# Fourteen idle products during the weight load, and a new issue order planned with later transpose landings

## The chip, the cores and the metric

The kernel runs on one core of a Trainium2 chip. The metric is device time in microseconds (us) of one execution. Before the change the median of five runs was 1848.56 us, from 1846.41 to 1852.45.

## What is computed

The input `x` has 2048 rows of 512 numbers. Four blocks follow one another, A, B, A, B, each added to its own input after a layernorm. All weights are shared between the two layers.

```python
def _A_ref(x, mem0, Wq, Wk, Wv, Wo, seg_len):      # 32 heads of 128, M = 8, seg_len = 32
    mem = mem0
    for s in range(n_seg):                          # 64 segments
        xs = x[:, s * seg_len:(s + 1) * seg_len, :]
        h = jnp.concatenate([mem, xs], axis=1)      # 40 rows
        q, k, v = (jnp.einsum('btd,dhe->bhte', h, W) for W in (Wq, Wk, Wv))
        p = softmax(where(mask, q k^T * scale, -1e9))
        o = jnp.einsum('bhte,hed->btd', p v, Wo)
        mem = o[:, :M, :]                           # the next segment's first 8 rows
        outs.append(o[:, M:, :])

def _B_ref(x, wqkv, wo):                            # linear attention, 32 heads of 16
    ...
    kv = jnp.einsum('bhsd,bhse->bhde', pk, v)       # summed over all 2048 rows
    ...
```

Block A is a recurrence: the eight memory rows of a segment are the first eight output rows of the segment before it. So 64 segments in each of two layers, 128 in all, follow one another. Block B needs a sum over all rows before any of its outputs can be made.

## The kernel before

**Work.** The weights of block A stay in SBUF (`Wq_sb`, `Wk_sb`, `Wv_sb`, 4 MB each, and `Wo_sb`). They are loaded at the start: the ACT queue issues the loads of Wq, Wk and Wv one after the other, and the SP queue issues four loads of Wo, two of them only when Wk has landed and two when Wv has landed. `wqkv` of block B follows on SP after the last of Wo.

A tile `t` (or `G`) is 128 rows of x, so four segments. A segment `s` multiplies a block of 32 rows: 8 memory rows and the first 24 of its own rows. The 8 rows that are left of each of the four segments of a tile are put together as a "left" block of 32 rows and done once a tile, ahead of need (`left_block`). Heads are done in two halves `b`. The steps of a segment:

- `turned` projects a block by Wq or Wk (through `project`, L777: 16 products of 32 columns by 512, four to a PSUM tile's four column groups), copies the result to an image `img` in SBUF (L608 on ACT or L609 on DVE), and turns it to have the head's dimension on the partitions. For half 0 of segments 1 to 62, and for both halves of the left block, the turning is a DMA transpose issued from SP (L790). For the others it is 16 transposing products (L799) and a copy. The image ring has three places for the segments' own images (marked urgent), and a fourth place alone for the left block, so the next left image can be copied only when the last one's transpose has landed.
- `project` by Wv gives `vimg`.
- `mem_attention(s, b)` makes the memory rows' attention: scores (L861), exponential, masks, sums (L878), and the product with v (L891, L892).
- `out_block` multiplies by Wo (L987, in `out_proj`), `next_mem` (L1012) turns the result into the next segment's memory rows in `hT`.
- `x_attention` (L916, L932, L935, L959, L960) and `residual` (L1029) do the other rows. `left_block` has the left block's own scores at L827. `prepare` does the layernorm (L738 to L750) of the next tile and its left block.
- `b_in`, `b_mid` and `b_out` are block B's parts, put between the segments; `b_mid` and the work around it stand alone between the layers.

**Order.** Nothing is issued in the order in which it is written. Each operation becomes a node with a cost in us; a node that issues a DMA has also a landing time `lat`. `_Prog.schedule` then goes through simulated time: each engine takes, among the nodes that are ready by the plan, the one with the highest priority. The priority of a node is

```python
                step, name, k = nd.key
                nd.prio = -(step * PERIOD + OFFSET[name][k])
```

so the table `OFFSET` is the order: some 350 numbers, one for each operation of a segment, written out. `MODE_SLACK` says how much priority TensorE gives away to stay in the same tiling mode of the array, and `LOOK` for how long it is kept free for a product of higher priority that is about to be ready. The planner also gives out the eight PSUM banks. What it yields is a fixed order of instructions on each engine, with semaphore waits where one engine needs another. On the chip each engine goes through its list in order; the plan's times do not exist there, only the order does. An instruction that waits holds up all behind it on its engine.

**What the plan assumed of DMAs.** A transpose is held to occupy SP for 1.25 us and to land `TURN` = 1.8 us later, so 3.05 us from its issue. The loads of rows of x are held to land 2.0 us after their issue. The weights are held to land 13.2, 23.7 and 34.8 us after theirs.

Of the kernel before, what the change touches and what calls it, by code (L numbers as in the profile page):

```python
# [16 lines left out]
HOP = 0.06  # L17
PE_SWITCH = 0.1
TURN = 1.8
MODE_SLACK = 12.41  # L20

LOOK = 0.074

PERIOD = 13.5
OFFSET = {
    "ld0": (3.45,),
    "ld1": (4.20,),
    "ld2": (-0.95,),
    "ld3": (-2.85,),
    "ld4": (0.40,),  # L30
    "startF": (12.05,),
    "prepF": (-11.05, 4.70, -9.25, -18.05, -7.00, -0.35, -15.95, -12.35, -15.40, 1.00, -1.65),
    "left0F": (-15.70, 1.30, -14.50, 0.25, -0.65, -12.60, 1.65, 6.55),
    "left1F": (15.35, 7.60, -6.60, 4.95, -3.45, 3.20, -0.65, 3.10),
    "leftv0F": (-1.70, -10.10),
    "leftv1F": (9.60, 0.00),
    "leftsF": (3.55, 9.85, 9.35, 1.25),
    "xlF": (1.05,),
    "qk0F": (0.15, 4.00, 2.75, -11.15, 1.55, 1.85, 11.40, 4.05),
    "qk1F": (0.00, -3.50, -2.10, -1.25, -25.90, -0.00, -5.45, 1.95),  # L40
    "v0F": (10.40, 1.50),
    "v1F": (31.95, 7.50),
    "mem0F": (2.55, 0.25, 5.85, -8.30, -1.20, -6.05, 2.15, 3.05, -1.60),
    "mem1F": (17.30, 12.60, 0.00, 1.10, -1.45, -6.00, -2.05, -21.65, 0.45),
    "outF": (1.85, -6.05, -5.85, -2.60),
    "nextF": (-0.45, -5.40, 13.70),
    "xF": (8.05, 1.50, -5.55, 5.05, -0.25, 9.95, 19.65, 5.95, -2.30, 7.20, 8.70, -12.05, -8.75, 4.00, -1.15,
        37.05, 0.30, 2.95, 10.30, 7.45, -2.10, 1.40, 0.10),
    "qk0": (-14.10, 1.50, -0.25, -5.35, -0.10, -0.05),
    "qk1": (1.55, 4.60, -0.05, -0.60, 1.80, 0.00, 7.10, -0.45),  # L50
    "v0": (0.35, -0.20),
    "v1": (5.15, 3.10),
    "mem0": (-5.20, -2.15, -1.60, -49.45, -13.55, -22.95, -3.35, -7.90, 4.70),
    "mem1": (7.10, -4.05, 3.25, -3.75, -2.90, 12.50, 5.15, -16.25, -12.15),
    "out": (-0.75, 4.95, 2.15, 0.00),
    "next": (1.75, 2.45, -4.05),
    "res": (48.90, 6.30, 2.30, -15.10, -1.45, -7.60, -2.50),
    "x": (2.45, 5.90, -2.85, -0.45, 6.20, 0.00, 15.70, -4.55, -22.30, 6.10, -15.10, 5.80, -2.55, 10.75, 6.10,
        0.60, 3.80, 21.60, 10.55, 5.20, 22.60, 29.30, 0.00),
    "prep": (7.35, -10.90, 1.30, 0.30, 10.40, -17.80, -4.90, 5.95, -3.00, -10.50, 9.70),  # L60
    "left0": (-4.00, -0.25, 18.45, -8.00, 1.40, -0.65),
    "left1": (0.10, 3.65, 0.45, 20.95, 3.05, -3.60),
    "leftv0": (32.60, 0.10),
    "leftv1": (11.30, 2.45),
    "lefts": (-2.95, 4.00, 0.50, -7.85),
    "xl": (6.35,),
    "bi": (0.25, -5.75, -1.85, -4.15, 6.60, -10.30, 9.70, -1.75, -6.35, 0.00, -15.35, 2.10, 7.40, -0.60, 21.85,
        -3.30, -3.50, 3.75, 0.00, 7.95, 2.05, 2.85, 12.85),
    "qk0L": (-9.45, 1.80, -2.10, 2.25, -3.65, 4.55, -0.30, 0.30),
    "qk1L": (-2.85, -6.75, -3.35, 4.40, -6.30, 2.10, -0.10, -1.70),  # L70
    "xL": (-6.30, -9.90, -7.95, -2.90, -3.60, 0.00, 4.70, 0.70, -2.85, 14.90, -19.10, 0.15, -0.20, 1.10, 6.60,
        0.15, -2.50, -0.30, -0.90, 0.00, -4.35),
    "lr": (-0.80, 7.55, 8.15, -13.30, 0.15, 7.95),
    "outL": (15.55, 3.95, 0.40, 10.10),
    "resL": (1.40, 4.60),
    "biL": (4.55, -5.70, -1.45, -34.70, -5.20, 0.75, 5.85, -1.90, -1.35, 0.15, 2.50, -24.50, -0.65, -21.55,
        1.05, 0.00, 0.00, 5.40, -1.60, -1.10, 11.15, -3.20, 3.85),
    "bm": (-3.95, -5.05, 16.55, 0.70, -0.20, 3.70, -9.00, 16.45, 0.15, -8.55, 2.25, 4.05, 2.75),
    "boF": (0.00, 7.10, -11.80, 3.35, 0.85, 0.75, -24.50, -13.85),
    "bo": (-1.10, 6.15, -2.70, -2.90, 0.00, -11.50, 1.10, -9.70),  # L80
    "ldL": (22.20, 1.70),
    "boL": (-26.60, 4.05, -1.85, -7.50, -5.65, -6.10, -13.50),
    "boZ": (18.15, -34.85, -14.20, 0.00, 8.30, -5.35, -7.10),
}


# [12 lines left out]
def c_pe(n_mm, n):  # L99
    return n_mm * max(0.0255, (n / 2.4 + 3.0) * 1e-3)  # L100
# [390 lines left out]
def _build_kernel(nc, A_x, A_mem0, A_Wq, A_Wk, A_Wv, A_Wo, A_seg_len, B_wqkv, B_wo, out):  # L491
# [34 lines left out]
    x_sb = sb("x_sb", [128, NX, D])  # L526
# [93 lines left out]
    o_view = out[0].rearrange("(t p) d -> t p d", p=128)  # L620
    qk_view = [W.rearrange("(c p) h e -> p c (h e)", p=128) for W in (A_Wq, A_Wk, A_Wv)]

    def x_move(o, i, k, reads, writes, kind, eng="pool"):
        add(eng, lambda e: e.dma_start(o, i), 1.1 if eng == "pool" else 0.4, reads=reads, writes=writes,
            dsem="%s%d" % (kind, k), lat=2.0)

    shift = [0]

    def slot(t):

        return (t + shift[0]) % NX
# [1 line left out]
    P.at(-9000, "ld0")  # L633
    add("sp", lambda s: s.dma_start(mem0_sb[0:M, :], A_mem0[0]), 0.1, writes=[MEM0], dsem="dmem", lat=2.0)
    P.at(-8000, "ld1")
    add("sp", lambda s: s.dma_start(x_sb[:, 0, :], x_view[0]), 0.4, writes=[("x", 0)], dsem="dx0", lat=2.0)
    late = []
    for i, (W, v, nm, t) in enumerate(((Wq_sb, qk_view[0], "Wq", 13.2), (Wk_sb, qk_view[1], "Wk", 23.7),
                                       (Wv_sb, qk_view[2], "Wv", 34.8))):
# [81 lines left out]
    def _m0(t, tl=tl):  # L721
        for c in range(4):
# [3 lines left out]
    evac(memT0_sb[:, :, :], lambda tl=tl: tl.bf16()[:, 0:4 * M].rearrange("p (c m) -> p c m", m=M), 32, tiles=[tl],  # L726
         writes=["memT0"])


    ln_no = [0]  # L730

# [30 lines left out]
    def a_layer(base, first):  # L762
# [20 lines left out]
        def turned(W, key, blk, bkeys, b, dst, dkey, urgent, dma):  # L783

            tl = project(W, key, blk, bkeys, b, urgent)
            k = img_no[0] % NI if urgent else NI
            img_no[0] += urgent
            nd = evac(img[:, k, :], lambda: tl.f32()[:, :], 512, tiles=[tl], writes=[("img", k)], urgent=urgent)
            if dma:
                add("sp", lambda e: e.dma_start_transpose(dst.rearrange("p h j x -> p h (j x)"), img[:, k, :]), 1.25,  # L790
                    reads=[("img", k)], writes=[dkey], dsem="turn%d" % k, lat=TURN)
                return nd
            tt = P.tile()

            def tr(pe):
                for i in range(4):
                    for j in range(4):
                        o = 128 * i + 32 * j
                        r = pe.transpose(tt.bf16()[32 * j:32 * j + 32, 128 * i:128 * i + 128], img[:, k, o:o + 32],  # L799
                                         id_sb[:, :], tile_position=(0, 32 * j))  # L800
                return r
            add("pe", tr, c_pe(4, 128), reads=[("img", k), "id"], tiles=[tt], urgent=urgent, mode="col")
            evac(dst.rearrange("p h j x -> p (h j x)"), lambda: tt.bf16()[:, 0:512], 512, tiles=[tt], writes=[dkey],
                 rate=2, urgent=urgent)
            return nd
# [193 lines left out]
        def out_block(s):  # L999
            at(s, "out")  # L1000
            keys = [[("oTm", s % NO, b), ("oTx", s % NO, b)] for b in range(2)]
            return out_proj(oTb[:, s % NO, :, :], keys, True)
# [61 lines left out]
        def tokens(t, s):  # L1064

            if not first:
                b_out(base + s, t, 0)
            elif t:
                at(s, "xl")
                x_move(x_sb[:, slot(t), :], x_view[t], slot(t), [], [("x", slot(t))], "dxl")  # L1070

        at(-4, "start")
        evac(hT[:, 0, 0, :, 0:8], memT0_sb[:, :, :], 32, reads=["memT0"], writes=[("hTm", 0, 0)])
# [3 lines left out]
        for s in range(NSEG):  # L1077
            G, g = divmod(s, 4)
            r2 = s % 2
            blk = hT[:, G % 2, g, :, :]  # L1080
            bk = [("hTm", G % 2, g), ("hTx", G % 2, g)]
            if g == 0 and G + 1 < NT:
                tokens(G + 1, s)
            for b in range(2):
                at(s, "qk%d" % b)
                hs = slice(4 * b, 4 * b + 4)
                turned(Wq_sb, "Wq", blk, bk, b, qT[:, r2, hs, :, :], ("qT", r2, b), True, QDMA[b] and 0 < s < NSEG - 1)
                turned(Wk_sb, "Wk", blk, bk, b, kT[:, r2, hs, :, :], ("kT", r2, b), True, KDMA[b] and 0 < s < NSEG - 1)
            for b in range(2):
                at(s, "v%d" % b)  # L1090
                tl = project(Wv_sb, "Wv", blk, bk, b, True)
                evac(vimg[:, r2, 512 * b:512 * b + 512], lambda tl=tl: tl.f32()[:, :], 512, tiles=[tl],
                     writes=[("v", r2, b)], urgent=True)
            if s + 1 < NSEG:
                for b in range(2):
                    mem_attention(s, b)
            w_of[s] = out_block(s)
            if s + 1 < NSEG:
                next_mem(s, w_of[s])
            if s > 0:  # L1100
                residual((s - 1) // 4, (s - 1) % 4, w_of[s])
                if g == 0:
                    b_in(base + s + 2, G - 1, not first)
            x_attention(s)
            if g == 2 and G + 1 < NT:
                prepare(G + 1, s)
            if s == NSEG - 1:
                at(s, "lr")
                add("pool", lambda p: p.memset(oTl[:, :, 24:32], 0.0), 0.5, writes=[("oTl", b) for b in range(2)])
                left_rows(NT - 1)  # L1110
# [206 lines left out]
```

The softmax here doesn't subtract the row's maximum and nothing guards it: scores larger than these inputs give would overflow.

## Time and profile before

| what | value |
|---|---|
| median of five runs | 1848.56 us |
| the profiled execution | 1852.73 us |
| its span, first to last instruction | 1851.0 us |
| around the span | 1.7 us |
| mean granted TensorE clock | 0.989 |
| PE busy | 1759.0 us, 95% of the span |
| ACT, DVE busy | 1207.7 us, 1017.4 us |
| matrix products recorded | 46693 |
| DMA transposes | 368 |

The profile is one execution. PE is TensorE's products, PEld its weight loads, DVE VectorE, ACT ScalarE, POOL GpSimd, SP the queue that issues the transposes. "L790" is line 790 of the kernel before. The lines of the helpers stand for many operations: L608 and L609 are nearly all copies out of PSUM on ACT and DVE. `arena_sb` is the one SBUF tensor that holds all working buffers, so a wait for `arena_sb` must be told apart by its line.

The span has four parts: the start (0 to about 100 us, in which the weights land), 64 segments of the first layer up to about 905 us, some 20 us between the layers in which one operation waits for the other, 64 segments of the second layer up to about 1811 us, and an end of 40 us.

### The profile page before, as it was taken

How to read it: one execution, taken by the hardware profiler on the slowest of the kernel's cores; microseconds unless marked ns; L12 is line 12 of the kernel's file. 1: busy time of each engine (PE TensorE's matmuls, PEld its weight loads, DVE VectorE, ACT ScalarE, POOL GpSimd, SP SyncE). 2: the span in 40 equal slices, each digit the busy share in tenths (PEclk: the TensorE clock that was granted, in tenths of full speed). 3: DMA queues.
4: the chain of work that ended last, by engine and by line, in shares of the span. 5: the costliest groups of instructions: out<-in, count | busy, mean ns of one | idle time of the engine just before them, and what ended most of it. 6: DMA issues, size and time to landing. Idle time of an engine off the chain costs nothing.

```text
span 1851.0 us, 100858 instructions
## 1 busy us (share of the span) xinstructions
PE 1759.0 (95%) x46693; PEld 1195.3 (65%) x46693; DVE 1017.4 (55%) x3168; ACT 1207.7 (65%) x3127; POOL 77.0 (4%) x182
## 2 busy tenths in 40 slices
PE   5899999999999999999799999999999999999997
PEld 2566666666667666666566666666766666666663
DVE  2355555555555555555545555556555566555565
ACT  3566666766666666666466667666667666667665
POOL 3000000000000000000000000000000000000000
PEclk9999999999999999999899999999999999999998
DMA  9322121212221222211011222122222222122222
GB/s 366 83 39 40 40 41 35 47 37 44 37 38 43 35 46 38 41 40 38 22 26 41 37 38 49 37 41 44 40 37 49 39 45 41 41 42 43 51 64 95
DMA packets 218934, 94.85 MB, mean 51 GB/s; under 512 B 202536, under 2 KB 212656, under 8 KB 216976
## 3 DMA queue, kind: packets, MB, share of 16 engines
q1 hardware_dynamic: 211312, 60.22, 17.9%
q0 software_dynamic: 5616, 15.60, 2.8%
q10 hardware_dynamic: 1584, 12.58, 1.7%
q8 instruction: 365, 5.98, 1.4%
q14 instruction: 57, 0.47, 0.1%
HBM read 29.63 MB, written 10.49 MB: 22 GB/s over the span
## 4 chain that ended last, share of the span: by engine, by line
PE 81%; DMA 13%; ACT 3%; DVE 2%; issue 1%; SPq 0%; ACTq 0%; DVEq 0%
PE pb L777 36%; PE pb L987 16%; DMA arena_sb<-arena_sb 10%; PE pb L861 3%; PE pb L959 3%; PE pb L1029 3%; PE pb L799 3%; PE pb L1137 3%; ACT arena_sb L608 2%; PE pb L916 2%; PE pb L878 2%; PE pb L1173 1%; DMA Wk_sb<-in_A_Wk_dram 1%; PE pb L892 1%; PE pb L891 1%; PE pb L1255 1%
## 5 line engine op out<-in xcount | busy, mean ns | idle before, releaser
L608 ACT ACTIVATE arena_sb<-pb 128x512 bf16<-128x512 f32 (+6 forms) x1412 | 726.8, 523 | 363.1 <-PE pb L777 300.0
L777 PE MATMUL pb<-Wq_sb,arena_sb 128*32 128x512 bf16 x5120 | 357.4, 383 | 0.7 <-DMA Wq_sb<-in_A_Wq_dram 0.6
L777 PE MATMUL pb<-Wv_sb,arena_sb 128*32 128x512 bf16 x5120 | 354.8, 380 | 0.6 <-issue 0.6
L777 PE MATMUL pb<-Wk_sb,arena_sb 128*32 128x512 bf16 x5120 | 344.2, 382 | 6.3 <-DMA Wk_sb<-in_A_Wk_dram 5.5
L987 PE MATMUL pb<-Wo_sb,arena_sb 128*32 128x256 bf16 x10368 | 327.3, 273 | 9.2 <-issue 3.9
L987 PEld LDWEIGHTS pb<-Wo_sb,arena_sb 128*32 128x32 bf16 x10368 | 261.8, 96 | 38.7 <-DVE arena_sb L895 13.2
L944 DVE TENSOR_TENSOR arena_sb<-arena_sb 32x256 bf16<-32x256 bf16 x512 | 213.2, 416 | 120.4 <-ACT arena_sb L940 109.3
L609 DVE CAST arena_sb<-pb 128x128 bf16<-128x128 f32 (+3 forms) x334 | 118.4, 355 | 252.5 <-PE pb L1012 200.7
L609 DVE COPY arena_sb<-pb 128x512 bf16<-128x512 bf16 (+2 forms) x352 | 137.6, 392 | 210.9 <-PE pb L799 205.6
L777 PEld LDWEIGHTS pb<-Wk_sb,arena_sb 128*32 128x32 bf16 x5120 | 142.3, 97 | 125.7 <-DMA Wk_sb<-in_A_Wk_dram 5.6
L777 PEld LDWEIGHTS pb<-Wq_sb,arena_sb 128*32 128x32 bf16 x5120 | 133.5, 97 | 114.0 <-DVE arena_sb L609 24.1
L777 PEld LDWEIGHTS pb<-Wv_sb,arena_sb 128*32 128x32 bf16 x5120 | 134.3, 97 | 85.0 <-issue 2.4
L608 ACT ACTIVATE outW_sb<-pb 128x128 fp32r<-128x128 f32 x261 | 72.4, 277 | 116.7 <-PE pb L987 77.4
L799 PEld LDWEIGHTS pb<-id_sb,arena_sb 128*32 128x32 bf16 x4352 | 77.3, 97 | 96.3 <-ACT arena_sb L608 65.2
L959 PE MATMUL pb<-arena_sb 128*128 128x128 bf16 x1024 | 131.3, 217 | 0.3 <-DVE arena_sb L946 0.3
L799 PE MATMUL pb<-id_sb,arena_sb 128*32 128x128 bf16 x4352 | 109.7, 221 | 19.6 <-ACT arena_sb L608 19.1
L946 DVE TENSOR_TENSOR arena_sb<-arena_sb 32x64 bf16<-32x64 bf16 x512 | 111.0, 217 | 15.8
L960 PE MATMUL pb<-arena_sb 128*128 128x32 bf16 x1024 | 118.7, 178 | 0.0
L868 ACT ACTIVATE arena_sb<-pb 128x256 bf16<-128x256 f32 x252 | 96.1, 383 | 29.4 <-PE pb L861 22.8
L861 PE MATMUL pb<-arena_sb 128*128 128x32 bf16 x2016 | 96.9, 178 | 6.9 <-DMA arena_sb<-arena_sb 6.7
L861 PEld LDWEIGHTS pb<-arena_sb 128*128 128x128 bf16 x2016 | 74.7, 96 | 31.4 <-DMA arena_sb<-arena_sb 7.8
L895 DVE TENSOR_TENSOR arena_sb<-pb,arena_sb 128x128 bf16<-128x128 f32 x252 | 72.2, 286 | 40.1 <-ACT arena_sb L883 27.6
(121 smaller groups left out, 2307.9 us busy)
## 6 DMA issues: line engine op xcount, KB each, us to landing
arena_sb<-arena_sb SPq DMA_TRANSPOSE x368, 2.5
Wq_sb<-in_A_Wq_dram ACTq DMA_DIRECT2D x1, 4096.0 KB, 13.6
Wk_sb<-in_A_Wk_dram ACTq DMA_DIRECT2D x1, 4096.0 KB, 24.4
Wv_sb<-in_A_Wv_dram ACTq DMA_DIRECT2D x1, 4096.0 KB, 34.8
Wo_sb<-in_A_Wo_dram SPq DMA_DIRECT2D x4, 1024.0 KB, 11.7
xs_scratch<-x_sb POOLq DMA_DIRECT2D x32, 128.0 KB, 2.1
pq_scratch<-arena_sb POOLq DMA_DIRECT2D x32, 128.0 KB, 2.8
x_sb<-xs_scratch POOLq DMA_DIRECT2D x16, 128.0 KB, 2.4
```

The source lines that it names most:

```text
L608: return e.activation(o() if callable(o) else o, i() if callable(i) else i, ACTF.Copy)
L609: return e.tensor_copy(o() if callable(o) else o, i() if callable(i) else i)
L777: r = pe.matmul(tl.f32()[32 * j:32 * j + 32, 0:512], blk[:, c, :], W[:, c, o:o + 512], start=(c == 0), stop=(c == 3), tile_position=(0, 32 ...
L799: r = pe.transpose(tt.bf16()[32 * j:32 * j + 32, 128 * i:128 * i + 128], img[:, k, o:o + 32], id_sb[:, :], tile_position=(0, 32 * j))
L861: r = pe.matmul(tl.f32()[:, o:o + 32], kk[:, hh, :, :].rearrange("p j x -> p (j x)"), qT[:, r2, hh, :, 0:8], start=True, stop=True)
L868: add("act", lambda a: a.activation(Pm[:, k, :, :].rearrange("p a q -> p (a q)"), tl.f32()[:, 0:256], ACTF.Exp, scale=SCALE), c_act(256), ...
L895: add("dve", lambda v: v.tensor_tensor(oTb[:, s % NO, 16 * b:16 * b + 16, 0:8], pv.f32()[:, 0:128].rearrange("p (n q) -> p n q", q=8), Rm[ ...
L944: add("dve", lambda v, q=q, j=j: v.tensor_tensor(Pbx[q, :, j, 0:32], Px[q, :, :], Rx[q, :, :], ALU.mult), c_dve(256) + 0.075, reads=["Px", ...
L946: add("dve", lambda v, q=q, j=j: v.tensor_tensor(Pbx[q, :, j, 32:40], PLL[q, g2, :, gl], Rx[q, :, 0:8], ALU.mult), c_dve(64) + 0.075, read ...
L959: pe.matmul(o, vimg[:, r2, e], Pbx[:, hh, :, 0:32], start=True, stop=False)
L960: return pe.matmul(o[:, :, 0:8], vleft[:, g2, e], Pbx[:, hh, :, 32:40], start=False, stop=True)
L987: r = pe.matmul(tl.f32()[32 * j:32 * j + 32, 0:256], oT[:, 4 * hh + n, :], Wo_sb[:, 8 * n + hh, 256 * d:256 * d + 256], start=(hh == 0 and ...
```

## The change

**The products.** After the second node of `mem_attention(0, 1)`, the scores against kT of the very first segment, fourteen products are added. Each has 32 columns of the identity as its weights and 512 columns of Wq as its moving operand, all in one column group of one PSUM tile. Nothing reads the result. Their priority is -2000, so in the plan PE takes them only when it has nothing else that is ready; they need PE, `id`, `Wq`, and one PSUM bank from the first to the last of them.

**The assumed landings.** A transpose is now held to land 0.2 us later when it is a segment's own and 0.6 us later when it is the left block's: 3.25 us and 3.65 us from issue. The first two loads of x are held to land 8.5 us after their issue and not 2.0. These numbers change nothing on the chip by themselves; they change what the planner puts where.

**The order.** Every number of `OFFSET` is new, and so are `MODE_SLACK` and `LOOK`. No operation of the computation is added or taken away.

```diff
-MODE_SLACK = 12.41
+MODE_SLACK = 29.57
 
-LOOK = 0.074
+LOOK = 0.055
 
 PERIOD = 13.5
 OFFSET = {
...
-    "mem0F": (2.55, 0.25, 5.85, -8.30, -1.20, -6.05, 2.15, 3.05, -1.60),
+    "warm": (2000.00,),
+    "mem0F": (3.95, -0.55, -1.40, -2.60, -33.00, 21.50, -6.90, -14.80, -1.80),
...
-    "qk0": (-14.10, 1.50, -0.25, -5.35, -0.10, -0.05),
-    "qk1": (1.55, 4.60, -0.05, -0.60, 1.80, 0.00, 7.10, -0.45),
+    "qk0": (-23.70, 0.00, 0.80, -6.15, 1.50, 2.10),
+    "qk1": (2.90, 1.80, -13.45, 4.95, 1.10, 6.10, -0.00, -5.35),
...
-    "left0": (-4.00, -0.25, 18.45, -8.00, 1.40, -0.65),
-    "left1": (0.10, 3.65, 0.45, 20.95, 3.05, -3.60),
+    "left0": (-0.50, 3.85, -5.00, -2.55, -3.35, 0.30),
+    "left1": (-5.30, -12.45, -0.35, -5.85, -0.70, -2.25),
...
-    "lefts": (-2.95, 4.00, 0.50, -7.85),
+    "lefts": (-7.25, 1.75, 2.50, -1.30),
...
 }
...
-    add("sp", lambda s: s.dma_start(x_sb[:, 0, :], x_view[0]), 0.4, writes=[("x", 0)], dsem="dx0", lat=2.0)
+    add("sp", lambda s: s.dma_start(x_sb[:, 0, :], x_view[0]), 0.4, writes=[("x", 0)], dsem="dx0", lat=8.5)
...
+    def warm(step, n, after):
+
+        P.at(step, "warm")
+        tl = P.tile()
+        for i in range(n):
+            if i:
+                P.again()
+            add("pe", lambda pe: pe.matmul(tl.f32()[0:32, 0:512], id_sb[:, 0:32], Wq_sb[:, 0, 0:512], start=True, stop=True,
+                                           tile_position=(0, 0)),
+                c_pe(1, 512), reads=["id", "Wq"], tiles=[tl], mode="col", after=after if i == 0 else ())
...
-                    reads=[("img", k)], writes=[dkey], dsem="turn%d" % k, lat=TURN)
+                    reads=[("img", k)], writes=[dkey], dsem="turn%d" % k, lat=TURN + (0.2 if urgent else 0.6))
...
-                x_move(x_sb[:, slot(t), :], x_view[t], slot(t), [], [("x", slot(t))], "dxl")
+                x_move(x_sb[:, slot(t), :], x_view[t], slot(t), [], [("x", slot(t))], "dxl", lat=8.5 if t == 1 else 2.0)
...
+            if first and s == 0:
+                warm(0, 14, [n for n in P.nodes if n.key == (0, "mem1F", 1)])
```

## The prediction

> **What bounds the kernel now.** I read the page first, its busy times, slices and chain:
>
> ```profile
> span 1851.0 us, 100858 instructions
> PE 1759.0 (95%) x46693; PEld 1195.3 (65%) x46693; DVE 1017.4 (55%) x3168; ACT 1207.7 (65%) x3127; POOL 77.0 (4%) x182
> PEclk9999999999999999999899999999999999999998
> PE 81%; DMA 13%; ACT 3%; DVE 2%; issue 1%; SPq 0%; ACTq 0%; DVEq 0%
> ```
>
> TensorE is the bound: busy for 95% of the span and 81% of the chain that ended last. The next engine, ACT, stands at 65%. So a change of order gains only where it fills idle time of PE, or lowers the time that PE loses between products of different kinds. How much is idle, and where, comes from busy times by stretch. The second row of the two below is the same for the second layer:
>
> ```profile
> 100.00:900.00 800.00, 779.62 (x21420) 540.53 (x21416) 442.74 (x1401) 542.17 (x1442) 25.24 (x47) 1.00 0.21 39
> 1000.00:1800.00 800.00, 782.65 (x21088) 538.64 (x21076) 462.15 (x1464) 538.90 (x1380) 31.10 (x57) 1.00 0.22 42
> ```
>
> The first number after the length is PE: 20.4 us idle in the first layer's stretch and 17.35 in the second's, 37.7 together, at the full clock. The rest of PE's 92 us of idle time (1851.0 less 1759.0) is 28.4 in the first 100 us, 11.3 in 900 to 1000, 14.6 after 1800. The last two are chains of single operations between and after the layers, which an order cannot shorten much. So the order can win at most about 38 us in the layers, plus something at the start. The waits of PE in the first stretch, longest in sum first, and L827's of the second, show what the 37.7 are:
>
> ```profile
> PE pb L799 <- ACT arena_sb L608: 5.9, 11, 0.8
> PE pb L861 <- DMA arena_sb<-arena_sb: 5.1, 6, 1.1
> PE pb L827 <- DMA arena_sb<-arena_sb: 3.1, 5, 0.9
> ...
> PE pb L827 <- DMA arena_sb<-arena_sb: 4.9, 7, 1.1
> ```
>
> (us in sum, times, longest). L827 waits for transposes of the left block, L861 for those of the segment's own images. L799 waits for a copy on ACT, and I followed each of these one step back: 14 of 23 such copies had themselves waited for the landing of a transpose, because an image place was still being read. By the semaphores each belongs to a segment's own image. In the two stretches, L827 lost 8.1 us (12 times), L861 6.7 (8 times), L799 behind ACT 9.5 (14 times): 24.3 of the 37.7 us of idle time in the layers come from transposes that landed late.
>
> The row of the transposes says how late:
>
> ```profile
> L790 SPq DMA_TRANSPOSE arena_sb<-arena_sb x368: 1188/1210/2526, 37.0 to 1783.1; - x184
> DMA to landing us min/median/max: 2.4/2.5/6.5
> ```
>
> The median, 2.5 us from issue, is under the 3.05 of the old plan. But counted one by one the landings fall in two groups: 210 of 368 are under 2.7 us, and 87 are over 3.65, most between 3.9 and 4.4. All 158 that are over 2.7 overlap with a packet of the instruction queue (the page's queue q8, 365 packets, 5.98 MB); of the 210 fast ones 75 do. So the plan is right or generous for two in three, and about 1 us short for one in four. The chain passes through 46 transposes, 43 of them in the two stretches, none of these under 3.3 us.
>
> **The landings and the order.** The old margin was 3.05 us; the new is 3.65 for the left block's and 3.25 for a segment's own. A consumer that the plan puts 0.6 or 0.2 us later finds that much less of the wait, if other products stand in between, and with PE 97.6% busy in the layers they nearly always do. Taken wait by wait, min(wait, 0.6) over L827's thirteen (one more lies at 975 us) sums to 7.1 us; min(wait, 0.2) over L861's eight is 1.6 and over L799's fourteen 2.7. That is 11.4 us at most from these waits. From below: nothing, if the order only moves them, since which transposes meet an instruction packet is drawn anew with the order. I take the left block's in full, 7.1, as nothing in the recurrence waits for a left block that is worked a tile ahead, and half of the segment's own, 2.2, since those are in the recurrence. Sum: -9.3.
>
> The segment's own transposes can also cost. In 62 segments of each layer the plan now has the memory scores 0.2 us later, at most 124 x 0.2 = 24.8 us if every one were the bound. The chain passes through a transpose in 43 segments; there PE waits anyway, and a later place costs nothing that isn't lost already. I take 0, cover being the products of other segments and tiles, and use the 43 for the rival below.
>
> What every other number of the table does cannot be read from the trace. The remaining 13.4 us of idle time in the layers (37.7 less 24.3) are redrawn too; half of it, 6.7, either way is my bound for that, and 0 the value.
>
> **The loads of x.** The row of DMA issues gives the first load of x 8.5 us to landing, 2.0 assumed. Correcting it moves work on DVE and ACT before 13 us. The first product by Wq starts at 14.47, as Wq lands, after the layernorm's copies. What hides it is that load, and if a later place of the copies ate into it, the cost would be at most the 0.9 us that PE waits for the second tile's transposes at 13.29. I take 0.
>
> **The fourteen products.** Each is a 512-column product. The costliest such row, L777's, has four at once in about 0.216 us (0.86 us for 16 in the chain); alone in one column group each takes one such time, so 14 x 0.216 = 3.0 us at the full clock, and 6.0 at half. What they fill is read from the start:
>
> ```profile
> 25.00:31.05 6.05, 5.34 (x64) 2.29 (x68) 0.42 (x1) 1.19 (x2) 0.00 (x0) 0.50 1.01 416
> 31.05:37.00 5.95, 5.32 (x182) 2.96 (x175) 3.04 (x11) 3.28 (x7) 0.00 (x0) 1.00 1.03 381
> 37.00:44.00 7.00, 4.54 (x89) 2.19 (x89) 3.44 (x13) 4.00 (x12) 0.00 (x0) 1.00 1.16 283
> 44.00:50.00 6.00, 5.43 (x114) 2.92 (x115) 0.58 (x2) 3.88 (x8) 0.00 (x0) 1.00 0.93 227
> 55.00:61.80 6.80, 3.53 (x80) 1.52 (x68) 0.42 (x1) 2.24 (x5) 0.78 (x1) 1.00 0.97 259
> 61.80:68.60 6.80, 6.64 (x148) 4.46 (x152) 2.18 (x8) 3.70 (x12) 0.00 (x0) 0.50 0.41 100
> ```
>
> (PE, PEld, DVE, ACT, POOL, then the granted clock, DMA share, GB/s.) The clock is at half in two places: until 31.05, after PE had waited 5.5 us for Wk; and from 61.8 to 68.6, after PE had waited 3.35 us at 61.88 for a copy behind a transpose that took 6.5 us while `wqkv` loaded. The products come after the first and before the second: their condition, the scores against kT, ends near 36 us, Wv lands at 36.6, Wo at 49.5. In between the clock is full already, with 3.1 us of PE idle from 31.05 to 44 (0.63 and 2.46), of which 0.3 lies before their condition (a wait at 33.99), so 2.8, and 0.6 more to 50. So they have no half clock of this trace to mend. If the idle time takes them all they cost 0; if the K projections end late, as they do at half clock (5.34 us of work at 0.50 is 2.7 late), they delay the Wv products by up to 3.0 us on PE. I take 1.5, the middle, both ends being equally near. What is queued behind them on PE is the first segment's v, its output product and so the second segment; the Wo wait of 0.57 at 49.74 is the first cover.
>
> The Trainium skill ("TensorE: Matmul & The Clock Gate", the section on why this matters) asks for no idle gaps of over about 3 us between bursts of products, and so would give products in gaps of 1.4 us no worth at all. A row here is stricter than that: PE waited 1.76 us at most before 1212 us, with 6.24 of the 8 us before it busy, and from 1212.1 to 1215.5 the clock was at half. By the page the term is 0 to +3.0 us; by that row the products may also save such a dip, 1.7 us or, at the length of the one at 61.8, 3.4, and the term is -3.4 to +3.0.
>
> **The sum.** Against the profiled execution's 1852.73 us: -9.3 for the late landings, 0 for the loads of x, +1.5 for the products, -7.8 in all, 1844.9. That execution is 4.2 us above the median of the runs, so on the median 1848.56 - 7.8 = 1840.8, say 1841.
>
> **The rivals.** *Slower: the recurrence.* Where the chain passes through a segment's memory scores, later places make each such segment longer. A segment takes 13.3 us and has 0.3 us of idle PE in it (37.7 over some 120 segments), so there is hardly any slack to give back. Place: L861 and what follows it to L1012. Price: 0.2 us for each of the 43 segments in which the chain passes a transpose, 8.6, and 3.0 for the products, with no wait shortened: +11.6, 1860. It decides once the other products of the plan run out before the 3.25 us do; for it speaks that L861's eight waits have none of them another product behind which to hide, against it that 281 of 368 landings are under 3.65 and the products after them need not wait.
>
> *No change.* The instruction packets hit as many transposes as before and the waits of 24.3 us come back under other lines, the products cost 0 to 3.0: 1848.6 to 1851.6, say 1850. For it: the added 0.2 us is far from the 1 us that is lacking.
>
> *More than forecast.* All 11.4 us of waits go, and the order keeps the transposes of the second segment away from the load of `wqkv`: the 3.35 us wait and the half clock behind it (6.8 us at 0.50, 3.4) go too: 1848.6 - 11.4 - 6.7 = 1830. Nothing in the change aims at the latter.
>
> *The change isn't what it says:* the fourteen products could lie in the plan where PE is not idle. Then they are 3.0 us of plain cost, which lies in the no-change case.
>
> **How the numbers follow.** 0.2%, 3.7 us, is about what a measurement of this kernel can tell from no change, so faster means under 1844.9 and slower over 1852.3. Forecast 0.41 (1841; its own range 1834 to 1848, the unknown 6.7 to each side, so about 0.04 of it is in the middle band), more than forecast 0.13, no change 0.12, recurrence and other losses by the redrawn order 0.34. Faster: 0.37 + 0.13 = 0.50; same: 0.12 + 0.04 = 0.16; slower: 0.34. The range from 1830 to 1862 leaves out half of the better case and some of the slower one where the 6.7 comes on top of 1860.
>
> **What would show it.** PE's waits for transposes in the two stretches fall from 24.3 to about 15 us, L827's from 8.1 to about 1; PE idle there from 37.7 to about 28. The landings keep their two groups, some 80 to 95 over 3.65 us. The chain passes fewer than 46 transposes. The clock between 31 and 55 us is full, as it was. Fourteen products by `id_sb` and `Wq_sb` stand between 33 and 50 us, and the product at 49.74 does not start over 1.5 us later. I am wrong if L827's waits stay, if idle PE in the layers grows, or if the span changes by what happens before 100 us.

## The result, and the profile after

The changed kernel takes 1844.76 us (median of 35 runs, 1838.93 to 1851.34), the kernel before 1848.74 us (59 runs beside them). The ratio is 0.9977, with a 95% interval of 0.9970 to 0.9984: 4.3 us less by the ratio (the medians differ by 4.0), just past the 0.2% that can be told from no change. 1841 was predicted.

The page after, lines as of before:

```profile
span 1844.7 us, 100785 instructions
PE 1762.0 (96%) x46707; PEld 1197.0 (65%) x46707; DVE 1092.0 (59%) x3259; ACT 1169.1 (63%) x3036; POOL 76.8 (4%) x182
PE 80%; DMA 13%; ACT 3%; DVE 2%; issue 1%; SPq 0%; ACTq 0%; DVEq 0%
```

Busy PE grew by 3.0 us, which is what fourteen products take (14 x 0.216). Idle PE, as the sum of the gaps between products, fell from 89.0 to 79.8 us. The span fell by the difference, 6.3 us; the two executions lie a little further apart than the medians. The stretches of the two layers:

```profile
100.00:900.00 800.00, 786.32 (x21514) 546.20 (x21514) 483.86 (x1472) 519.50 (x1378) 25.23 (x47) 1.00 0.23 40
1000.00:1800.00 800.00, 781.66 (x21122) 537.08 (x21117) 493.01 (x1484) 526.76 (x1365) 30.85 (x57) 1.00 0.23 45
```

PE is idle for 13.7 and 18.3 us there, 32.0 in place of 37.7. But these stretches lie at fixed times, and the changed kernel ends 6.3 us sooner, so that a wait of 1.7 us from the end of the work falls into its second stretch. PE's waits at the product by Wo behind "issue" (us, times, longest): before in 1800 to 1851, then after in 1000 to 1800 and in 1800 to 1851:

```profile
PE pb L987 <- issue: 3.7, 2, 1.9
```

```profile
PE pb L999 <- issue: 1.7, 1, 1.7
...
PE pb L999 <- issue: 1.6, 1, 1.6
```

Cut at the same places of the work (the last 51 us of each span for the end, and from 20 us ahead of `b_mid`'s first L1198, which is L1212 after, to 80 us behind it for the part between), the layers have 7.5 us less idle time (37.9 to 30.3), the start 2.4 less (28.4 to 26.0), the part between the layers 1.8 more (11.1 to 13.0) and the end 1.1 less (14.6 to 13.5). The lines of the code have moved: L873 is the old L861, L811 the old L799, L839 the old L827, L802 the old L790. PE's waits in the first layer (us, times, longest), and the left scores' line L839 in the whole kernel:

```profile
PE pb L873 <- DMA arena_sb<-arena_sb: 5.9, 11, 1.2
PE pb L811 <- ACT arena_sb L609: 2.8, 6, 0.8
PE pb L811 <- DVE arena_sb L610: 1.8, 4, 0.6
```

```profile
L839 PE MATMUL pb<-arena_sb x1024: 176/176/234, 33.8 to 1745.4; 128*32 128x32 bf16 x171
its engine sat idle before it (us, times) until:
who waited for it (us, times):
```

The list of what PE sat idle for ahead of L839 is empty; ahead of L827 it had been `DMA arena_sb<-arena_sb: 18.9, 26`, weight loads and products together. The waits for the segments' own transposes did not shrink: L873 has 8.9 us in the two stretches (6.7 before; all waits over 0.1 us counted, where the view starts at 0.15), L811 behind a copy behind a transpose 10.0 (9.5). So 24.3 us of waits for transposes became 19.0: the left block's 8.1 are gone, 2.8 came back on the segments' own.

The landings:

```profile
L802 SPq DMA_TRANSPOSE arena_sb<-arena_sb x368: 1188/1264/2550, 35.3 to 1777.7; - x184
DMA to landing us min/median/max: 2.4/3.0/8.4
```

101 of 368 are over 3.65 us (87 before), 62 of them segments' own (39 before). 199 are over 2.7 us (158 before). All 101 met a packet of the instruction queue; of the 199, 24 met none and landed after 2.9 to 3.4 us, 19 of these with a transfer `xs_scratch<-x_sb` in flight.

### The profile page after: what moved, and what is told of

Same layout as the page of the kernel before. It is cut to its first block, busy times and chain, and to the rows that moved or that the text cites. A ratio compares the mean times of both kernels' runs of the same rounds, so it can differ in the third digit from the quotient of the medians.

```text
span 1844.7 us, 100785 instructions
## 1 busy us (share of the span) xinstructions
PE 1762.0 (96%) x46707; PEld 1197.0 (65%) x46707; DVE 1092.0 (59%) x3259; ACT 1169.1 (63%) x3036; POOL 76.8 (4%) x182
## 4 chain that ended last, share of the span: by engine, by line
PE 80%; DMA 13%; ACT 3%; DVE 2%; issue 1%; SPq 0%; ACTq 0%; DVEq 0%
PE pb L789 35%; PE pb L999 16%; DMA arena_sb<-arena_sb 10%; PE pb L873 3%; PE pb L971 3%; PE pb L1151 3%; PE pb L811 3%; PE pb L1041 3%; PE pb L928 2%; PE pb L890 2%; ACT arena_sb L609 2%; PE pb L1187 1%; DMA Wk_sb<-in_A_Wk_dram 1%; PE pb L904 1%; PE pb L903 1%
## 5 line engine op out<-in xcount | busy, mean ns | idle before, releaser
L609 ACT ACTIVATE arena_sb<-pb 128x512 bf16<-128x512 f32 (+6 forms) x1365 | 674.1, 504 | 379.1 <-PE pb L789 326.3
L610 DVE CAST arena_sb<-pb 128x512 bf16<-128x512 f32 (+3 forms) x438 | 207.7, 475 | 357.8 <-PE pb L789 157.3
L789 PE MATMUL pb<-Wv_sb,arena_sb 128*32 128x512 bf16 x5120 | 361.7, 381 | 0.3 <-issue 0.3
L789 PE MATMUL pb<-Wq_sb,arena_sb 128*32 128x512 bf16 x5120 | 344.9, 381 | 1.3 <-ACT arena_sb L609 0.7
L789 PE MATMUL pb<-Wk_sb,arena_sb 128*32 128x512 bf16 x5120 | 317.9, 380 | 5.4 <-DMA Wk_sb<-in_A_Wk_dram 5.4
L999 PE MATMUL pb<-Wo_sb,arena_sb 128*32 128x256 bf16 x10368 | 311.0, 274 | 5.2 <-issue 3.3
L609 ACT ACTIVATE outW_sb<-pb 128x128 fp32r<-128x128 f32 x233 | 64.6, 277 | 170.8 <-PE pb L999 149.1
L610 DVE COPY arena_sb<-pb 128x512 bf16<-128x512 bf16 (+2 forms) x295 | 112.2, 396 | 67.1 <-PE pb L811 63.4
L873 PE MATMUL pb<-arena_sb 128*128 128x32 bf16 x2016 | 104.4, 178 | 13.1 <-DMA arena_sb<-arena_sb 11.6
L811 PEld LDWEIGHTS pb<-id_sb,arena_sb 128*32 128x32 bf16 x4352 | 69.6, 96 | 65.7 <-ACT arena_sb L609 40.3
L811 PE MATMUL pb<-id_sb,arena_sb 128*32 128x128 bf16 x4352 | 97.5, 220 | 14.2 <-ACT arena_sb L609 8.6
L873 PEld LDWEIGHTS pb<-arena_sb 128*128 128x128 bf16 x2016 | 74.3, 96 | 53.8 <-issue 22.2
## 6 DMA issues: line engine op xcount, KB each, us to landing
Wq_sb<-in_A_Wq_dram ACTq DMA_DIRECT2D x1, 4096.0 KB, 13.7
```

The costliest lines, as they stand in the source:

```text
L609: return e.activation(o() if callable(o) else o, i() if callable(i) else i, ACTF.Copy)
L610: return e.tensor_copy(o() if callable(o) else o, i() if callable(i) else i)
L789: r = pe.matmul(tl.f32()[32 * j:32 * j + 32, 0:512], blk[:, c, :], W[:, c, o:o + 512], start=(c == 0), stop=(c == 3), tile_position=(0, 32 ...
L873: r = pe.matmul(tl.f32()[:, o:o + 32], kk[:, hh, :, :].rearrange("p j x -> p (j x)"), qT[:, r2, hh, :, 0:8], start=True, stop=True)
L999: r = pe.matmul(tl.f32()[32 * j:32 * j + 32, 0:256], oT[:, 4 * hh + n, :], Wo_sb[:, 8 * n + hh, 256 * d:256 * d + 256], start=(hh == 0 and ...
```

## Experiments

My theory: the order gains by placing the consumers of late transposes later, above all the left scores; the lateness comes from packets of the instruction queue; the products are free or nearly so. The rivals: the gain is a lucky draw of an order; a wait removed comes back elsewhere; the products work through the clock. Ratios are to the kernel before on the same chip, with 95% intervals.

**What makes a transpose late.** A kernel of its own, with the PE part

```python
e.wait_ge(s_t, 16 * N1)                  # 60 transposes have landed
for i in range(MM_LONG):                 # 800
    e.matmul(pb[:, :], x_sb[:, 1, 0:128], x_sb[:, 2, :], start=True, stop=True)
e.wait_ge(s_t, 16 * 2 * N1)
for i in range(MM_SHORT):                # 3600
    e.matmul(pb[:, 0:32], x_sb[:, 1, 0:128], x_sb[:, 2, 0:32], start=True, stop=True)
```

> A kernel that computes nothing of the reference: 180 DMA transposes of 128 by 512, each issued when the last has landed. During the first 60 PE is idle; during the next 60 it streams products of 512 columns; during the last 60 products of 32 columns, several times as many instructions in the same time. Theory (the late landings come from the packets of the instruction queue): first third all under 2.7 us; second third a tenth or so late; last third a quarter to a half late, each late one beside a packet of that queue. Rival (PE's reading of SBUF, or SP itself, holds them up): the second third as often late as the last, or late ones in the first.

PE (first after the length) in the three thirds, and then the instruction queue's packets, MB and share in the second and in the last third (there are none in the first):

```profile
9.00:154.00 145.00, 0.00 (x0) 0.00 (x0) 0.00 (x0) 1.00 0.27 54
154.50:304.00 149.50, 149.04 (x685) 67.32 (x686) 0.00 (x0) 1.00 0.27 52
305.00:490.00 185.00, 118.08 (x3712) 102.74 (x3710) 0.00 (x0) 0.85 0.37 45
```

```profile
q8 instruction: 5, 0.08, 0.2%
...
q8 instruction: 29, 0.48, 1.2%
```

Counted in the trace, 0, 5 and 29 of 60 transposes landed later than 2.7 us, and these are exactly those that overlap with one of the 0, 5 and 29 packets. The second third has the busier PE and the fewer late landings, so it is not PE's work that delays them. The theory holds for this kernel: a transpose that meets a packet of instructions lands late, at 3.2 to 4.1 us where 2.4 is the median, and no other does. In the large kernels packets are not the whole cause, as the 24 late landings of the changed kernel without one show.

**The left scores alone.** The kernel before, order kept, with L827's two nodes moved past the next four of PE in 30 tiles, and what reads them behind; the edit in short:

```diff
     P.schedule()
+    # in 30 tiles: the two PE nodes of "lefts" go behind the PE nodes planned within the next 0.9 us
+    for pe, anchor in left_scores(0.9):
+        for n in pe:
+            c.remove(n)
+        c[c.index(anchor):c.index(anchor)] = pe
```

> The kernel before, order kept, but in 30 tiles the left block's scores (L827, two nodes on PE) stand four nodes later on PE, by the plan 0.9 us or more, with the exponential that reads them behind. The number of changes of tiling mode stays 532. Theory of the prediction (each of L827's waits is idle PE that other products fill, 7.1 us in all): L827's waits fall from 8.1 us to under 2, PE's idle time by 6 to 7 us, and the ratio to before is 0.996 to 0.9975. Rival (a wait removed there comes back at the next late transpose, since the segments' chain is just as late): L827's waits fall too, those for the segments' own transposes grow by as much, and the ratio is 0.999 to 1.001.

Beside it the kernel before was profiled again on the same chip:

> The kernel before, profiled on the chip of this call, to set the profiles of the two kernels above beside one of the same chip. Any theory: the time of before on this chip, L827 waiting for late transposes for some 7 to 9 us, 532 changes of tiling mode.

The ratio is 0.9960 (0.9944 to 0.9976): 7.4 us. The span is 1835.6 us beside 1846.1. What PE's loads and products at L827 sat idle for (us, times), in the kernel before and then with the scores later:

```profile
  DMA arena_sb<-arena_sb: 17.9, 25
```

```profile
  DMA arena_sb<-arena_sb: 0.3, 2
```

PE's idle time fell by 7.3 us, from 96.0 to 88.7; cut at the same places of the work as above, it fell by 8.5 us in the layers (44.9 to 36.4), rose by 1.1 at the start and hardly changed elsewhere. The waits for the segments' own transposes stayed (13.4 and 13.6 us in the two stretches), so the rival that a wait comes back falls. By the ratios this one step gives as much as the whole change (0.9977) or more; the two intervals overlap, so that it gives more is not shown.

**Table and assumption apart.** The new table with the old landings; the old table with the new ones; and the changed kernel with the left block's landing alone put back:

```diff
...
-lat=TURN + (0.2 if urgent else 0.6))
+lat=TURN)                                  # new table, old landings; loads of x at 2.0 again
...
```

> The changed kernel with the old assumed landings put back (1.8 us for every transpose, 2.0 us for the loads of x) and the new table, slack and look kept; the products stay. Theory (the added 0.6 us for the left block is what took away the left scores' waits): L839 waits for transposes again, for some 5 to 9 us in the two stretches, and the time is 3 to 10 us over the changed kernel's. Rival (the table's new numbers made the gain, L839 is simply placed later by them): L839's waits stay under 1.5 us and the time is within 2 us of the changed kernel's.

> The kernel before with the new assumed landings alone (2.0 and 2.4 us for transposes, 8.5 us for the first loads of x); old table, slack and look, no products. Theory (assumed landings by themselves take the left scores' waits away): L827's waits fall from 8.1 us to under 2, and the time is 3 to 8 us under before. Rival (a table is fitted to its assumptions, and another assumption scrambles the order): L827's waits fall too or not, but other idle time of PE grows, and the time is at before's or up to 15 us over it.

> The changed kernel with the old assumed landing for the left block's transposes alone (1.8 us); the segments' own stay at 2.0. The order that the planner makes of it has 850 changes of TensorE's tiling mode where the changed kernel has 508 and before has 532. Theory (a table that is not searched for its assumed landings loses by such changes, 0.13 to 0.18 us each, as in the two mixed kernels): 44 to 62 us over the changed kernel, some 1880 to 1900 us, with PE's idle time up by under 15 us. Rival (what costs is L839's waits): L839 waits for 10 us or more, and the time is 10 to 20 us over the changed kernel's.

| table | assumed landings, own and left | ratio, or time | changes of tiling mode | L827 / L839 waits, two stretches |
|---|---|---|---|---|
| old | 1.8, 1.8 (before) | 1 | 532 | 8.1 |
| new | 2.0, 2.4 (changed) | 0.9977 | 508 | 0 |
| new | 1.8, 1.8 | 1.0364 (1.0347 to 1.0381) | 924 | 2.3 |
| old | 2.0, 2.4 | 1.0367 (1.0349 to 1.0386) | 1064 | 2.1 |
| new | 2.0, 1.8 | 1949.99 us (one run), 5.5% over the 1848.53 of before | 850 | 9.6 |

Of the first two I had expected 15 us over before at most; they are 68 and 67 us over it. PE shows no such wait. Its stretch from 100 to 900 us, in the new table with the old landings and in the old with the new:

```profile
100.00:900.00 800.00, 783.90 (x20784) 538.38 (x20785) 464.75 (x1380) 515.96 (x1382) 24.44 (x45) 1.00 0.20 39
```

```profile
100.00:900.00 800.00, 783.61 (x20728) 517.20 (x20725) 432.47 (x1380) 534.03 (x1380) 24.44 (x45) 1.00 0.20 39
```

PE is as busy as in the changed kernel (786.32), with 20784 and 20728 products where that does 21514. The loss lies inside the busy time: TensorE changes more often between products of 32 columns (forms 128*32) and of 128. In the first of the two the next product starts 150 ns later in the median after a change, within runs of 128-column products 26 (55 where they also move 128 columns). The first of the two is 75.6 us longer in span than the changed kernel profiled beside it, 18.4 of this idle; 57.2 us over 416 more changes is 0.14 us each. That it is the changes can be shown by adding up: the times from one product's start to the next's, waits included, sum to 191 us over its 924 changes and to 106 over the changed kernel's 508; over all other pairs of products they are 10 us less than there. For the second of the two the same division, less the 3.0 us of products that it lacks, gives 0.11 us. For the left landing alone I forecast 44 to 62 us from this and measured 106 over the changed kernel (taken as 0.9977 of before): 342 changes make some 48, and idle PE is 125.7 us for 79.8 in the changed kernel's profile (another chip), 46 more, of which L839's waits are 9.6. Both forecasts were too low. The left scores do wait less with the longer landing assumed, in the new table (0 us, against 2.3 and 9.6) and in the old (2.1, against 8.1). But 2.3 is less than the 5 to 9 that I had forecast, and orders that differ so much don't show what the landing does by itself. As a step by itself it isn't worth having: each table loses 3.6% under the other's assumptions.

**A draw of chance.** The changed kernel with 0.01 us more on each landing, called the nudged kernel below:

> The changed kernel with 0.01 us more for each assumed landing of a transpose (0.21 and 0.61 where it has 0.2 and 0.6), which can mean nothing for margins. It measures how far the time moves when the planner's choices fall otherwise by chance. Theory that the planned margin made the gain: within 1.5 us of the changed kernel. Rival that this is one lucky draw of an order: slower than the changed kernel by 3 us or more, L839's waits for transposes remaining near 0 in both cases.

0.9982 (0.9971 to 0.9993), and 0.9974 (0.9963 to 0.9985) for the changed kernel itself run again on the chip of the two mixed kernels. The order differs in hundreds of places on PE, ACT and DVE (538 changes of mode), the time hardly does: a second draw with the same table gains about as much, so the gain isn't one lucky draw of the planner's choices.

> The changed kernel as it is, run beside the next three on one chip, so that they can be set against it without the differences between chips. Both theories: a ratio to before of 0.997 to 0.9985.

**The products.** They are left out where instructions are written out:

```diff
                     for si, v in nd.waits:
                         e.wait_ge(self.sems[self.names[si]], v)
+                    if nd.key is not None and nd.key[1] == "warm":
+                        assert not nd.sig
+                        continue
                     ins = nd.fn(e)
```

> The changed kernel's order with the fourteen products left out at the place where instructions are written out, so that all else keeps its order and its waits. Theory (the products lie in idle time and cost nothing, the gain is the order's): the same time as the changed kernel within 1.5 us, a ratio to before of 0.997 to 0.999; the first output product still starts near 49.9 us, as Wo lands. Rival 1 (they keep the clock up): without them PE is idle for some 3 us more between 35 and 39.4 us, the clock falls to half for 3.4 or 6.8 us, and the time is 1.7 to 3.4 us longer than the changed kernel's. Rival 2 (they delay): up to 3.0 us shorter.

The ratio is 0.9962 (0.9950 to 0.9974). The stretch of the value weights and the first output product, changed kernel first:

```profile
37.00:44.00 7.00, 7.00 (x110) 3.35 (x110) 3.61 (x12) 3.52 (x10) 0.00 (x0) 1.00 1.17 275
```

```profile
49.92 1.93 PE L999 MATMUL pb<-Wo_sb,arena_sb 128*32 128x256 bf16 x64 [0.69 <-DMA Wo_sb<-in_A_Wo_dram]
```

```profile
37.00:44.00 7.00, 6.17 (x93) 2.61 (x93) 3.62 (x12) 3.38 (x9) 0.00 (x0) 0.76 1.17 281
```

```profile
38.49 4.46 PE L792 MATMUL pb<-Wv_sb,arena_sb 128*32 128x512 bf16 x48
...
49.70 0.51 PE L1002 MATMUL pb<-Wo_sb,arena_sb 128*32 128x256 bf16 x12 [0.52 <-DMA Wo_sb<-in_A_Wo_dram]
```

Without them the clock does fall to half, from 38.80 to 42.21 us, and the 48 products by Wv take 4.46 us. So they do keep the clock up; what I read from one profile of before, that there was nothing to keep up, was chance: before's second profile has a half clock from 39.80 to 43.21 too. Of the six profiles of kernels with the products none has a half clock near 39 us, of the seven without them five do. But nothing is gained by it. The next thing that matters is Wo, and the first output product comes as Wo lands, 0.2 us earlier without the products than with them. Rival 1 falls. The ratio is not in the theory's 0.997 to 0.999 either; it lies where rival 2 has it. The nudged kernel ran beside this one, and its median is 2.7 us longer (1839.72 and 1836.98); in these two profiles busy PE is 3.0 us less without the products (1761.3 and 1758.3), idle PE only 0.4 more (73.8 and 74.2). So the products most likely cost 1 to 3 us, nearly their busy time. It isn't settled: the intervals overlap, and the nudged order is not the same order.

**The loads for block B.** In the changed kernel's profile the second segment's k transpose took 6.0 us beside the load of block B's output weights. The load moved on POOL's queue:

```diff
     P.schedule()
+    nd = [n for n in c if n.dsem == "dwoB1"][0]          # c = P.committed
+    c.remove(nd)
+    k = [i for i, n in enumerate(c) if n.eng == "pool" and n.key is not None and n.key[1] == "xl"][2]
+    c.insert(k + 1, nd)
```

> The changed kernel with one DMA moved on POOL's queue: the load of block B's output weights, which is first read at about 900 us, is issued after the load of the fourth later tile of x (beyond 150 us) and not at 55.98 us, where the second segment's k transpose took 6.0 us. Nothing else moves. Theory (that load is what holds the transpose up, and the half clock after the wait follows from it): the transpose lands in 2.4 to 4.4 us, the wait of 2.1 us at 62.15 shrinks below 0.7, the half clock from 62.66 to 69.48 goes, and the kernel is 3 to 5.5 us faster than the changed one: ratio to before 0.995 to 0.996. Rival (the transpose is slow by itself at the end of the weights' loading): it stays near 6 us and the ratio stays 0.9977.

The transpose landed after 4.1 us, the wait of 2.1 us became one of 0.2 at 61.12, and the clock stayed full:

```profile
61.80:68.60 6.80, 6.05 (x206) 4.45 (x202) 4.55 (x16) 3.52 (x13) 0.00 (x0) 1.00 0.05 11
```

(0.56 in that stretch of the changed kernel.) But the ratio is 0.9967 (0.9955 to 0.9979), 1 to 2 us under the changed kernel and not 3 to 5.5. The collision is a race: in the changed kernel's other profile the same transpose landed after 4.6 us and the clock did not fall. With the products left out as well:

> The changed kernel without the fourteen products and with the load of block B's output weights moved beyond 150 us on POOL's queue. If leaving out the products is worth something by itself (the 0.15% seen between two chips) and the moved load 1 to 2 us, it stands 3 to 5 us under the changed kernel of this same call; if the first was only the difference of two chips, 0.5 to 2.5 us under it. In both, no half clock between 60 and 70 us and one of 3.4 us near 39.

0.9959 (0.9943 to 0.9974), 3.0 us under the median of the changed kernel that ran beside it, at the lower edge of the first forecast, with the clock as forecast. The intervals overlap here too, and the moved load has a share in the 3.0, so what the products cost by themselves stays open. The same idea on the old order, where both transposes of the second segment collide with `wqkv`, which is there issued from SP behind them:

> The kernel before, with its two loads for block B issued later: wqkv from SP after the second segment's two transposes (they were issued at 54.65 and 56.04 with it in flight and took 6.5 and 5.7 us), the output weights on POOL after a later tile of x (beyond 150 us). Theory (those loads hold the transposes up): both land in 2.4 to 4.4 us, the wait of 3.35 us at 61.88 and the half clock from 61.8 to 68.6 go, 3.5 to 6.7 us less: ratio 0.9964 to 0.998. Rival (the work that waits there is given back by the layer's end): ratio above 0.999.

0.9991 (0.9979 to 1.0002): hardly anything. Both transposes landed in 2.4 and 2.5 us. But `wqkv` then ran from 57.1 to 64.6, the left block's transpose issued at 60.6 met it and took 6.1 us, and PE waited for that. From 45 to 80 us, the kernel before and then this one:

```profile
PE pb L799 <- ACT arena_sb L608: 3.2, 1, 3.2
```

```profile
PE pb L827 <- DMA arena_sb<-arena_sb: 3.0, 1, 3.0
```

The wait was moved, not removed, and with it a half clock of 3.4 us, which begins at 66.9 where it began at 63.7.

## Why the prediction was right, and where its steps were not

- **The bound.** Held: PE at 96%, and the gain of the two profiles is idle PE, 7.5 us of it in the layers when both are cut at the same places of the work.
- **The size.** -7.8 was forecast and -4.3 came, so the sum was too hopeful by nearly half. That 1844.76 lies just under the 1844.9 up to which I had called it faster is luck.
- **The left block's waits, -7.1.** The scores moved alone gave -7.4 (by the interval, -4.4 to -10.4); in the changed kernel the waits of 8.1 are gone. The reason that nothing in the recurrence waits for them held too: nothing came back.
- **The segments' own waits, -2.2.** The step that failed. They went from 16.2 to 19.0 us, +2.8. I had shortened each old wait by the added 0.2 us, as if the same transposes would be late. The new order has other ones late, 62 of the segments' own over 3.65 us for 39. In the changed kernel's second profile they are 50 and the waits 14.1 us; before's second has 13.4. So this term scatters by as much as I gave it. That the waits grew is not shown; that they did not shrink by 2.2 is what both pairs of profiles show.
- **The loads of x, 0.** Held as far as seen: the first product by Wq starts at 14.56 us (14.47), with Wq's landing.
- **The products, +1.5.** They take 3.0 us of busy PE, with 2.4 us less idle time at the start, +0.6 by this pair of profiles; the runs without them point to 1 to 3 us, in which the middle that I took lies. The first output product is 0.2 us later, inside the range. The Trainium skill's rule of about 3 us between bursts ("TensorE: Matmul & The Clock Gate", the section on why this matters) would have made them useless for the clock. With them gone the longest gap before the half clock was 1.6 us, so this case differs from the rule, and the row of 1212 us was the better guide to the clock; neither said that Wo's landing hides the loss.
- **The sum.** -7.5 in the layers (-8.1 at the left scores, +2.8 at the segments' own, -2.2 at all else), +0.6 at the start, +1.8 between and -1.1 at the end make the 6.3 us of the two spans. The idle time between the layers stands in no term: three profiles of the changed and nudged orders have 12.7 to 13.4 us there, three with the old order there 11.1 to 11.3, so it goes with the new order.
- **The clock.** Also in no term: the runs' granted clocks average 0.992 for the changed kernel and 0.991 for the kernel before beside it on one chip, some 5 us less at half clock, which by this estimate could be up to 2.5 us of the gain. No run separates this from the rest. With the left scores moved the average stayed at 0.991, so it has no part in those 7.4 us.
- **What I left out.** Changes of tiling mode stand in no term. They are 508 for 532 here, some 3 us at 0.14 each, not to be seen in the busy time of this pair. In the first two mixed kernels they are the main cost.
- **The rivals.** The slower one, the longer recurrence, did not come about: L873 waited for a transpose 17 times in the two stretches, not in every segment, and the chain passes 45 transposes (46).
- **The signs.** L827's waits (0, "about 1"), the chain, the clock between 31 and 55 us and the product at 49.92 came as forecast. Idle time in the stretches fell less (32.0, "about 28"), so did the waits for transposes (19.0, "about 15"), and the landings did not keep their two groups: 169 are under 2.7 us for 210, and 101 over 3.65, not 80 to 95.

## What to carry to other kernels

Where an engine's idle time ends in a DMA, look at all its landings, not the median: here one in four was late by over 1 us, and moving the one consumer that had slack by four places won 7.4 us, no less than a new order of everything. An order and the assumptions that it was planned with belong together: changing the assumptions or the table alone cost 3.6%. Before idle time is added up by stretches of two profiles, see that the stretches hold the same work. And before a load is moved out of the way of one wait, look at what it will meet next.

## What the hardware showed that I had not expected

- A DMA transpose that overlaps with one packet of the instruction queue (16 KB) lands later, up to 4.1 us in place of 2.4, in 34 of 34 cases in the small kernel. In the kernel before all of the 158 over 2.7 us had met one; so had 75 of the 210 others. In the changed kernel 24 of the 199 over 2.7 us had met none; all of these landed within 3.4 us.
- TensorE's clock fell to half at 38.80 us after a stretch whose longest gap was 1.6 us, with PE busy for 5.3 of the 8 us before. In two profiles of the kernel before, of one and the same order, it fell near 39.8 us in one and not in the other.
- A change between products of 32 and of 128 columns costs 0.11 to 0.14 us of PE in these kernels, which the profile shows as busy.
